# Attention and a mixture of experts on one core: a GpSimd drain in mid-run, row stores by SyncE, and a fixed order in the small experts

## The chip, the cores and the metric

One core of a Trainium2 chip runs the whole program. Its engines are TensorE (matmuls, PE in the profile; PEld are its weight loads), VectorE (DVE), ScalarE (ACT), GpSimd (POOL) and SyncE (SP), each with an instruction queue of its own that runs in order; they wait for each other through semaphores. DMAs are issued by SyncE and GpSimd. The metric is the device time of the program in microseconds.

## The reference

What is computed, cut to what matters: capped softmax attention over 8 x 12 heads with 448 rows of 64, then a mixture of 8 experts in which each of the 3584 rows goes to one expert.

```python
scores = cap * np.tanh(scale * q @ k.T / cap)
attn = softmax(scores)                        # per batch (8) and head (12), 448 x 448
x = (attn @ v), heads side by side            # 3584 rows of 768
logits = x @ w_gate + modality_bias[modality_id]
e_idx = np.argmax(logits, axis=1)
gate_w = softmax(logits)[row, e_idx]
for e in range(8):
    mask = e_idx == e
    h = np.maximum(x[mask] @ w1[e], 0.0)      # 768 -> 1024
    out[mask] = gate_w[mask, None] * (h @ w2[e])   # 1024 -> 768
```

## The kernel before

**Attention** (`attention`, lines 428 to 751) goes over 24 pairs of head pairs, `d`, with seven steps `s` each. A step has scores on TensorE, Tanh and Exp on ScalarE, sums of the weights on DVE, and the products with v on TensorE some steps later. Nearly all of it is pinned: `pin` keeps an instruction at its place in the program order of its engine. At the first step of a pair `fetch(d + 1)` queues three loads of 448 KB each (k and q twice, v once) on SyncE. In the fifth step `tokens(d - 3)` transposes a finished pair, scales it into the tile `xs`, and stores it to the DRAM tensor `xd` (line 580). Of these 24 stores 23 are issued by GpSimd and one, pair 20, by SyncE; the calls for the last two pairs (lines 745 and 746) name GpSimd themselves. GpSimd also writes the row map of the experts with indirect DMAs (line 282).

**Experts.** Rows are gathered per expert in blocks ("slots") of up to three tiles of 128 rows. A slot is `run_slot`: GpSimd gathers the next slot's rows (`gather`, line 801), `ffn1` multiplies with w1 for f = 0 to 7, `ffn2` with w2, ScalarE scales the result (line 940), and GpSimd stores each tile of rows with an indirect DMA (line 949). Weights come in as float32 through four buffers `raw` and are split into a high part (cast on ScalarE, line 820) and a low part (subtraction on DVE, line 821), which are single tiles per k (w1: `ah`, `al`; w2: `bh`, `bl`). A matmul is done as three products of such parts.

With these inputs there are eight slots of three tiles, then the branch of `finish` with slots of 2, 2 and 1 tiles. In a slot of fewer than three tiles (`n < TW`) ffn1 puts the high and the low part of the rows side by side, so that a PSUM bank holds two halves; `finish(ph, f)` inside ffn1 adds them into the tile `acc` (copy at line 885, sum at 886), applies Relu (887) and takes the low part (888). In these slots the w2 splits are called after ffn1 and are not pinned; the order in which they stand among ffn1's instructions is that of the scheduler. The splits of the next slot's w1 are pinned.

**End.** Behind the last store every engine executes a drain and a barrier (line 1219 in the profile, written by the framework); the same at the start has line 1211.

Of the kernel before, what the change touches and what calls it, by code (L numbers as in the profile page):

```python
# [66 lines left out]
FIXED = 7  # L67
# [15 lines left out]
class Program:  # L83
# [344 lines left out]
    def attention(self, firsts, rp, xp):  # L428
        tc, nc = self.tc, self.nc
        pe, pin, V = nc.tensor, self.pin, nc.vector  # L430
        with ExitStack() as st:
# [126 lines left out]
                        rec[:, i].unsqueeze(3).to_broadcast([CP, C, 2, E]), op=ALU.mult,  # L558
                    ))

            def tokens(d, queue=nc.gpsimd, *banks):
                xT, rec = kept.pop(d), recs[d]
                xs = xp.tile([CP, C, 4 * D], F32, name="xs", bufs=2)
                if banks:
                    tps = [pool.tile([128, 512], F32, name="tp", tag=tag) for pool, tag in banks]
                else:
                    tp = ps_x.tile([128, 2, 512], F32, name="tp", tag="xT")
                    tps = [tp[:, i] for i in range(2)]
                for i in range(2):
                    for c in range(C):  # L570
                        pin(pe.transpose(
                            tps[i][:CP, c * 128 : (c + 1) * 128], xT[:, i, c * CP : (c + 1) * CP], self.ident
                        ))
                dst = xs.rearrange("p c (i j d) -> p i c j d", i=2, j=2)
                norm = rec.unsqueeze(4).to_broadcast([CP, 2, C, 2, D])
                for i in range(2):
                    src = tps[i][:CP].rearrange("p (c j d) -> p c j d", c=C, j=2)
                    pin(V.tensor_tensor(dst[:, i], src, norm[:, i], op=ALU.mult))
                b, r = divmod(d, NU)
                put = queue.dma_start(  # L580
                    self.xd[b * S : (b + 1) * S, r * 4 * D : (r + 1) * 4 * D].rearrange("(p c) f -> p c f", c=C), xs
                )
                if queue is nc.sync:
                    self.last_sp = pin(put).ins
# [239 lines left out]
        for k in range(KC):  # L824
            self.split_w(self.load_raw(e, self.w1, k, FF), self.w1s[k], pin=True)

    def load_w2(self, e, raws=(), ks=range(FC), minus=None):
        for k in ks:
            raw = raws[k] if k < len(raws) else self.load_raw(e, self.w2, k, DM)
            self.split_w(raw, self.w2s[k], pin=bool(raws), minus=minus)  # L830

    def move(self, k, pt, n=TW):
        for t in range(n):
# [15 lines left out]
        self.move(k, pt, n)  # L849
        self.take(k, pt, n)  # L850

    def ffn1(self, n, hooks=None):

        nc = self.nc
        w = n * 128
        hh, hl = self.h
        bank = lambda: self.ps_h.tile([128, 512], F32, name="ph")
        lead = LEAD if hooks else 0

        def parts(k):  # L860
            hi, lo = self.w1s[k]
            for a, c in ((hi, 0), (lo, 0), (hi, 1)):
                for f in range(lead):
                    self.pin(nc.tensor.matmul(
                        phs[f][:, :w], a[:, f * 128 : (f + 1) * 128], self.x[:, k, c, :w],
                        start=k == 0 and a is hi and c == 0, stop=k == KC - 1 and c == 1,
                    ))

        def products(ph, f, k):
            hi, lo = self.w1s[k]  # L870
            keep = self.pin if hooks and f <= lead else (lambda inst: inst)
            fs = slice(f * 128, (f + 1) * 128)
            first, last = k == 0, k == KC - 1
            if n == TW:
                keep(nc.tensor.matmul(ph[:, :w], hi[:, fs], self.x[:, k, 0, :w], start=first, stop=False))  # L875
                keep(nc.tensor.matmul(ph[:, :w], hi[:, fs], self.x[:, k, 1, :w], start=False, stop=False))  # L876
            else:
                nc.tensor.matmul(ph[:, : 2 * w], hi[:, fs], self.x[:, k, :, :w], start=first, stop=False)
            keep(nc.tensor.matmul(ph[:, :w], lo[:, fs], self.x[:, k, 0, :w], start=False, stop=last))  # L879

        def finish(ph, f):
            acc = ph[:, :w]
            if n < TW:
                acc = self.op.tile([128, 256], F32, name="acc", bufs=2)[:, :w]
                nc.vector.tensor_copy(acc, ph[:, w : 2 * w])
                nc.vector.tensor_tensor(acc, ph[:, :w], acc, op=ALU.add)
            nc.scalar.activation(hh[:, f, :w], acc, AF.Relu)  # L887
            nc.vector.scalar_tensor_tensor(hl[:, f, :w], acc, 0.0, hh[:, f, :w], op0=ALU.max, op1=ALU.subtract)  # L888

        def hook(*at):  # L890
            if hooks and at in hooks:
                hooks[at]()

        if lead:
            hooks["start"]()
            phs = [bank() for _ in range(lead)]
            for k in range(KC):
                parts(k)
                if k < KC - 1:
                    hook("k", k)  # L900
            for f in range(lead):
                finish(phs[f], f)
            hook("k", KC - 1)
        for f in range(lead, FC):
            ph = bank()
            for k in range(KC):
                products(ph, f, k)
            finish(ph, f)
            hook("f", f)

    def ffn2(self, mt, n, between=(), wait=0, then=None):

        nc = self.nc
        between = list(between)
        for t in range(n):
            ot = self.op.tile([128, DM], F32, name="ot")
            rows = slice(t * 128, (t + 1) * 128)
            pys = {}

            def products(half, f):  # L920
                if f == 0:
                    pys[half] = self.ps_y.tile([128, 512], F32, name="py")
                cs = slice(half * HALF, (half + 1) * HALF)
                for i, (a, c) in enumerate(((0, 0), (0, 1), (1, 0))):
                    nc.tensor.matmul(  # L925
                        pys[half][:, :HALF], self.h[a][:, f, rows], self.w2s[f][c][:, cs],
                        start=f == i == 0, stop=f == FC - 1 and i == 2,
                    )

            both = wait and t == 0  # L930
            if both:
                for f in range(FC):
                    for half in range(2):
                        products(half, f)
            for half in range(2):
                if not both:
                    for f in range(FC):
                        products(half, f)
                cs = slice(half * HALF, (half + 1) * HALF)
                put = nc.scalar.mul(ot[:, cs], pys[half][:, :HALF], mt[:, t, 1:2])  # L940
                if both:
                    self.pin(put)
                    if half:
                        then()
                left = 2 * n - 1 - (2 * t + half)
                if 2 * t + half >= wait:
                    for _ in range(-(-len(between) // left) if left else 0):
                        between.pop(0)()
            nc.gpsimd.indirect_dma_start(  # L949
                self.out, bass.IndirectOffsetOnAxis(ap=mt.bitcast(I32)[:, t, 0:1], axis=0), ot, None,  # L950
                bounds_check=NT - 1, oob_is_err=False,
            )

    def run_slot(self, cur, n, ahead=None, raws=(), hooks=None):

        moves = []  # L960
        if hooks:
            work = hooks[("f", 3)]
            hooks[("f", 3)] = lambda: (work(), self.load_w2(cur[0], raws, range(W2_FIRST, W2_EARLY)))
        elif n == TW:
            self.load_w2(cur[0], raws)
        nxt = ahead() if ahead and not hooks else None
        self.ffn1(n, hooks)
        if hooks:
            self.load_w2(cur[0], raws, range(W2_EARLY, FC))
            nxt = ahead()  # L970
        if n < TW:
            self.load_w2(cur[0], raws)
        then = lambda: self.load_w1(nxt[0])
        if nxt:
            if not hooks:
                then()
            pool = lambda k: (self.ps_h, "ph") if hooks and k % 3 == 2 else (self.ps_t, "ptr")
            moves = [lambda k=k: self.transpose(k, *pool(k), n=nxt[2]) for k in range(KC)]
        self.ffn2(cur[1], n, between=moves, wait=3 if hooks else 0, then=then if hooks else None)
        return nxt  # L980

    def run_slots(self, cur, hooks):
# [4 lines left out]
        def ahead(i, n=TW):  # L987
            meta = self.meta
            if i == 0:
                maps.append(self.second)  # L990
                maps.extend(self.rows(meta, s, flex=s >= FIXED, after=self.got) for s in range(1, FIXED + 3))
            else:
                self.gather(maps[i], n)
            return self.expert(meta, i), maps[i], n

        for i in range(FIXED + 1):
# [227 lines left out]
```

## Time and profile before

| | us |
|---|---|
| median of 3 runs | 857.93 (856.28 to 858.07) |
| the profiled execution | 859.21 |
| its span, first to last instruction | 857.5 |
| TensorE busy | 831.3 |
| ScalarE busy | 532.2 |
| DVE busy | 509.0 |
| GpSimd busy | 147.0 |

The span is shorter than the time of the same execution by what lies around the first and last instruction. Busy time counts compute and GpSimd's DMA issues, no waits, drains, branches or semaphores; an engine can hold up the end in an instruction that isn't counted. In a timeline row the first number is the start in us from the start of the span, the second the duration, and the bracket at the end is the idle time of that engine just before, with what ended it. The attention stage lasts until about 330 us, the slots of three tiles until 754 us, the small ones from there.

### The profile page before, as it was taken

What the parts mean: (1) busy time and instruction counts of PE and PEld (TensorE: products, weight loads), DVE (VectorE), ACT (ScalarE), POOL (GpSimd) and SP (SyncE); (2) the same over time, 40 slices, a digit from 0 to 9 for tenths busy, and PEclk for the clock granted to TensorE, in tenths of its full rate; (3) what the DMA queues carried; (4) which work ended last, traced back from release to release, by engine and by line L of the source; (5) the groups of instructions that cost most, each with busy time, mean ns of one, the idle gap of its engine ahead of it and who ended that gap; (6) DMA issues with size and microseconds to landing.
All of it is one profiled execution on the core that took longest, in us unless ns stands there. A gap on an engine that the chain in (4) does not pass through costs nothing. (4 is left out here: it accounts for less than half of the span.)

```text
span 857.5 us, 15780 instructions
## 1 busy us (share of the span) xinstructions
PE 831.3 (97%) x6176; PEld 630.9 (74%) x6176; DVE 509.0 (59%) x880; ACT 532.2 (62%) x627; POOL 147.0 (17%) x154
## 2 busy tenths in 40 slices
PE   7999999999999989999999999999999999999995
PEld 2344434444434436999999999999999999989984
DVE  3677788877688788954433444443344423466851
ACT  6999999999999876364434434443344433456541
POOL 2000330033032230352020210203012030111000
PEclk9999999999999999999999999999999999999998
DMA  5344445365445674397352564634547353457640
GB/s 173 103 152 128 131 127 171 134 173 116 145 120 139 173 168 174 86 330 262 122 184 106 169 231 141 210 105 162 194 141 250 107 160 134 160 178 237 218 160 6
DMA packets 44388, 136.84 MB, mean 160 GB/s; under 512 B 8638, under 2 KB 9214, under 8 KB 44304
## 3 DMA queue, kind: packets, MB, share of 16 engines
q1 hardware_dynamic: 34576, 101.00, 36.8%
q0 software_dynamic: 9584, 34.74, 12.9%
q8 instruction: 50, 0.82, 0.4%
q14 instruction: 34, 0.28, 0.1%
q10 hardware_dynamic: 144, 0.00, 0.0%
HBM read 114.20 MB, written 22.69 MB: 160 GB/s over the span
## 5 line engine op out<-in xcount | busy, mean ns | idle before, releaser
L466 ACT ACTIVATE pt<-sc,isc 128x896 f32<-128x896 f32 x168 | 160.2, 996 | 14.6 <-PE sc L462 12.1
L925 PE MATMUL py<-bh,hh 128*128 128x384 f32 x464 | 160.0, 345 | 1.3 <-ACT hh L887 1.2
L879 PE MATMUL ph<-x,al 128*128 128x384 f32 (+2 forms) x510 | 160.0, 314 | 0.0
L925 PE MATMUL py<-bh,hl 128*128 128x384 f32 x464 | 156.4, 337 | 0.0
L925 PE MATMUL py<-bl,hh 128*128 128x384 f32 x464 | 156.3, 337 | 0.0
L469 ACT ACTIVATE pt<-pt,cabs 128x1792 f32<-128x1792 f32 x84 | 150.4, 1790 | 2.7
L492 PE MATMUL xT<-pt,va 64*64 64x448 f32 x1344 | 143.1, 540 | 3.5 <-issue 3.5
L480 DVE TENSOR_TENSOR tot<-tot,pt 128x896 f32<-128x896 f32 x120 | 130.3, 1086 | 7.8 <-ACT pt L469 4.6
L875 PE MATMUL ph<-x,ah 128*128 128x384 f32 x366 | 122.7, 335 | 1.2 <-DVE hl L888 1.1
L876 PE MATMUL ph<-x,ah 128*128 128x384 f32 x366 | 122.4, 334 | 0.0
L821 DVE TENSOR_TENSOR bl<-raw,bh 128x768 fp32r<-128x768 f32 x88 | 81.6, 955 | 51.6 <-ACT bh L820 51.5
L492 PEld LDWEIGHTS xT<-pt,va 64*64 64x64 f32 x1344 | 50.0, 133 | 82.6 <-issue 77.8
L820 ACT CAST bh<-raw 128x768 fp32r<-128x768 f32 x88 | 70.6, 841 | 52.5 <-DMA raw<-in_w_dram 49.8
L949 POOL DMA_INDIRECT out_dram<-ot,mt x29 | 32.0, 1102 | 382.1 <-ACT ot L940 310.0
L879 PEld LDWEIGHTS ph<-x,al 128*128 128x128 f32 x510 | 96.0, 188 | 0.0
L887 ACT ACTIVATE hh<-ph 128x384 fp32r<-128x384 f32 x64 | 30.2, 488 | 103.9 <-PE ph L879 99.0
L940 ACT ACTIVATE ot<-py,mt 128x384 f32<-128x384 f32 x58 | 33.6, 580 | 95.8 <-issue 49.9
L925 PEld LDWEIGHTS py<-bh,hh 128*128 128x128 f32 x464 | 87.0, 188 | 2.4 <-ACT hh L887 1.8
L821 DVE TENSOR_TENSOR al<-raw,ah 128x1024 fp32r<-128x1024 f32 x64 | 76.3, 1222 | 20.9 <-ACT ah L820 20.6
L925 PEld LDWEIGHTS py<-bh,hl 128*128 128x128 f32 x464 | 87.1, 188 | 0.1
L925 PEld LDWEIGHTS py<-bl,hh 128*128 128x128 f32 x464 | 87.1, 188 | 0.0
L845 DVE TENSOR_TENSOR x<-ptr,x 128x384 fp32r<-128x384 f32 (+2 forms) x63 | 31.0, 515 | 87.2 <-ACT x L844 82.6
(173 smaller groups left out, 1024.0 us busy)
## 6 DMA issues: line engine op xcount, KB each, us to landing
raw<-in_w_dram SPq DMA_DIRECT2D x88, 384.0 KB
raw<-in_w_dram SPq DMA_DIRECT2D x62, 512.0 KB
kq<-in_kq_dram SPq DMA_DIRECT2D x24, 448.0 KB
va<-in_v_dram SPq DMA_DIRECT2D x24, 448.0 KB
kx<-in_kq_dram SPq DMA_DIRECT2D x24, 448.0 KB
xd<-xs POOLq DMA_DIRECT2D x23, 448.0 KB, 6.2
raw<-in_w_dram POOLq DMA_DIRECT2D x2, 512.0 KB
spare<-in_w_dram POOLq DMA_DIRECT2D x2, 512.0 KB, 8.6
```

What stands on the lines that cost most here:

```text
L466: pin(nc.scalar.activation(weights(n), sc[:, :, :S], AF.Tanh, scale=self.isc))
L469: pin(nc.scalar.activation(pt, pt, AF.Exp, scale=self.cabs))
L480: pin(V.tensor_tensor(tots[d], pt_of(n - 1) if s == 1 else tots[d], pt_of(n), op=ALU.add))
L492: pin(pe.matmul(self.xT[j * D : (j + 1) * D, i, :S], vas[d][rows, o : o + D], pt[rows, j], start=s == 0, stop=s == STEPS - 1,))
L820: keep((cast.tensor_copy if cast else self.nc.scalar.copy)(hi, raw))
L821: keep((minus or self.nc.vector).tensor_tensor(lo, raw, hi, op=ALU.subtract))
L875: keep(nc.tensor.matmul(ph[:, :w], hi[:, fs], self.x[:, k, 0, :w], start=first, stop=False))
L876: keep(nc.tensor.matmul(ph[:, :w], hi[:, fs], self.x[:, k, 1, :w], start=False, stop=False))
L879: keep(nc.tensor.matmul(ph[:, :w], lo[:, fs], self.x[:, k, 0, :w], start=False, stop=last))
L925: nc.tensor.matmul(pys[half][:, :HALF], self.h[a][:, f, rows], self.w2s[f][c][:, cs], start=f == i == 0, stop=f == FC - 1 and i == 2,)
L940: put = nc.scalar.mul(ot[:, cs], pys[half][:, :HALF], mt[:, t, 1:2])
L949: nc.gpsimd.indirect_dma_start(self.out, bass.IndirectOffsetOnAxis(ap=mt.bitcast(I32)[:, t, 0:1], axis=0), ot, None, bounds_check=NT - 1, ...
```

## The change

- `tokens` has SyncE as its default queue instead of GpSimd. Its store is then pinned in SyncE's order.
- In the slot after the fixed eight (`i == FIXED + 1`) GpSimd executes a drain right behind the gather for the next slot.
- In slots of one or two tiles: the first four w2 tiles are loaded and split ahead of ffn1; the splits of the other four are called inside `finish` for f = 0 to 3, between sum and Relu, and pinned; the copy into `acc` goes from DVE to ScalarE; copy, sum, Relu and subtraction are pinned.
- In the last tile of the last slot the scaling of the second half is cut in two, one half by ScalarE and one by DVE.

```diff
-            def tokens(d, queue=nc.gpsimd, *banks):
+            def tokens(d, queue=nc.sync, *banks):
...
-    def load_w2(self, e, raws=(), ks=range(FC), minus=None):
+    def load_w2(self, e, raws=(), ks=range(FC), minus=None, pin=False):
         for k in ks:
             raw = raws[k] if k < len(raws) else self.load_raw(e, self.w2, k, DM)
-            self.split_w(raw, self.w2s[k], pin=bool(raws), minus=minus)
+            self.split_w(raw, self.w2s[k], pin=pin or bool(raws), minus=minus)
...
         def finish(ph, f):
             acc = ph[:, :w]
+            keep = self.pin if n < TW else (lambda inst: inst)
             if n < TW:
                 acc = self.op.tile([128, 256], F32, name="acc", bufs=2)[:, :w]
-                nc.vector.tensor_copy(acc, ph[:, w : 2 * w])
-                nc.vector.tensor_tensor(acc, ph[:, :w], acc, op=ALU.add)
-            nc.scalar.activation(hh[:, f, :w], acc, AF.Relu)
-            nc.vector.scalar_tensor_tensor(hl[:, f, :w], acc, 0.0, hh[:, f, :w], op0=ALU.max, op1=ALU.subtract)
+                keep(nc.scalar.copy(acc, ph[:, w : 2 * w]))
+                keep(nc.vector.tensor_tensor(acc, ph[:, :w], acc, op=ALU.add))
+            if f < len(inside):
+                inside[f]()
+            keep(nc.scalar.activation(hh[:, f, :w], acc, AF.Relu))
+            keep(nc.vector.scalar_tensor_tensor(
+                hl[:, f, :w], acc, 0.0, hh[:, f, :w], op0=ALU.max, op1=ALU.subtract
+            ))
...
-                put = nc.scalar.mul(ot[:, cs], pys[half][:, :HALF], mt[:, t, 1:2])
+                cut = HALF // 2 if last and t == n - 1 and half else HALF
+                put = nc.scalar.mul(ot[:, half * HALF :][:, :cut], pys[half][:, :cut], mt[:, t, 1:2])
+                if cut < HALF:
+                    nc.vector.tensor_scalar(
+                        ot[:, half * HALF + cut :], pys[half][:, cut:HALF], mt[:, t, 1:2], None, op0=ALU.mult
+                    )
...
-        self.ffn1(n, hooks)
+        inside = ()
+        if n < TW:
+            self.load_w2(cur[0], (), range(W2_EARLY))
+            inside = [lambda k=k: self.load_w2(cur[0], (), (k,), pin=True) for k in range(W2_EARLY, FC)]
+        self.ffn1(n, hooks, inside)
...
-        if n < TW:
-            self.load_w2(cur[0], raws)
...
                 self.gather(maps[i], n)
+                if i == FIXED + 1:
+                    self.pin(nc.gpsimd.drain())
```

`W2_EARLY` is 4, `FC` is 8, `HALF` is 384, `FIXED` is 7 and `TW` is 3.

## Rows read from the trace of the kernel before

**Rows 1.** Stages: us, busy PE, PEld, DVE, ACT, POOL, then clock, DMA, GB/s.
```profile
100.00:200.00 100.00, 99.80 (x1010) 41.34 (x1006) 80.01 (x150) 98.22 (x85) 22.84 (x22) 1.00 0.49 146
...
440.00:480.00 40.00, 40.00 (x236) 39.94 (x235) 19.77 (x25) 17.43 (x27) 4.49 (x4) 1.00 0.58 191
...
760.00:800.00 40.00, 39.08 (x228) 35.88 (x227) 31.31 (x55) 22.99 (x37) 3.92 (x4) 1.00 0.79 264
800.00:840.00 40.00, 37.95 (x249) 36.35 (x248) 27.02 (x58) 19.83 (x37) 1.99 (x2) 1.00 0.42 144
```

**Rows 2.** Timeline of TensorE, from the first and last small slot.
```profile
776.51 0.44 PE L925 MATMUL py<-bh,hh 128*128 128x384 f32 x1 [0.92 <-ACT hh L887]
...
828.47 0.22 PE L879 MATMUL ph<-x,al 128*128 128x128 f32 x1
828.52 0.34 PE L878 MATMUL ph<-x,ah 128*128 128x256 f32 x1
828.70 0.22 PE L879 MATMUL ph<-x,al 128*128 128x128 f32 x1
829.68 0.36 PE L878 MATMUL ph<-x,ah 128*128 128x256 f32 x1 [0.77 <-DVE acc L886]
...
832.22 0.35 PE L878 MATMUL ph<-x,ah 128*128 128x256 f32 x1 [0.95 <-DVE acc L886]
...
834.12 0.35 PE L878 MATMUL ph<-x,ah 128*128 128x256 f32 x1 [0.33 <-DVE acc L886]
```

**Rows 3.** Timeline of ScalarE, same two slots.
```profile
775.09 1.05 ACT L820 CAST ah<-raw 128x1024 fp32r<-128x1024 f32 x1 [1.22 <-PE py L925]
776.04 0.41 ACT L887 ACTIVATE hh<-acc 128x256 fp32r<-128x256 f32 x1
...
829.84 0.83 ACT L820 CAST bh<-raw 128x768 fp32r<-128x768 f32 x1 [1.50 <-DMA raw<-in_w_dram]
```

**Rows 4.** Timeline of all engines at the end of the run.
```profile
846.78 0.34 PE L925 MATMUL py<-bh,hl 128*128 128x384 f32 x1
847.15 0.58 ACT L940 ACTIVATE ot<-py,mt 128x384 f32<-128x384 f32 x1 [3.64 <-PE py L925]
848.01 0.98 POOL L949 DMA_INDIRECT out_dram<-ot,mt  x1 [21.31 <-POOLq L1008]
```

**Rows 5.** Line 1219: count, ns (least/median/most), first and last start.
```profile
L1219 POOLq DRAIN  x3: 50/109/5757, 850.9 to 857.2; - x3
L1219 SPq DRAIN  x3: 7/7/13, 851.4 to 856.9; - x3
```

**Rows 6.** Line 1211, the start of the program, same columns.
```profile
L1211 POOLq DRAIN  x1: 183/183/183, 0.5 to 0.5; - x1
```

**Rows 7.** Groups by line on GpSimd: count, busy us, mean ns, idle before.
```profile
L282 POOL DMA_INDIRECT mapd<-pay,pos x32 | 47.8, 1495 | 103.8 <-DVE pos L278 52.5 <-DVE xs L578 35.6 <-DVE early L311 8.3
L801 POOL DMA_INDIRECT xg<-xd,mt x30 | 36.7, 1224 | 38.2 <-PE ptr L834 20.8 <-DMA mt<-mapd 10.2 <-PE py L925 4.3
L949 POOL DMA_INDIRECT out_dram<-ot,mt x29 | 32.0, 1102 | 382.1 <-ACT ot L940 310.0 <-ACT x L844 50.2 <-POOLq L1008 21.3
L580 POOL DMA_DIRECT2D xd<-xs x23 | 16.7, 732 | 127.5 <-DVE xs L578 83.2 <-DVE lg L556 42.8 <-issue 1.2
L792 POOL DMA_DIRECT2D mt<-mapd x6 | 3.3, 550 | 2.8 <-issue 2.8
```

**Rows 8.** Timeline of GpSimd in the first small slot.
```profile
759.37 1.33 POOL L801 DMA_INDIRECT xg<-xd,mt  x1 [0.31 <-issue]
782.08 1.17 POOL L949 DMA_INDIRECT out_dram<-ot,mt  x1 [21.38 <-ACT x L844]
```

**Rows 9.** Line 580, the row stores: us from issue to landing.
```profile
DMA to landing us min/median/max: 5.6/6.2/6.7
```

**Rows 10.** Timeline of SyncE's queue in attention.
```profile
174.00 0.99 SPq L95 DMA_DIRECT2D kq<-in_kq_dram  x2
```

**Rows 11.** Timeline of TensorE, the first use of that load.
```profile
187.44 1.68 PE L462 MATMUL sc<-kq 64*64 64x448 f32 x16
```

More of the change, by code (lines that the diff above doesn't have):

```diff
@@ L850, in transpose, with ffn1 @@
         self.take(k, pt, n)
-    def ffn1(self, n, hooks=None):
+    def ffn1(self, n, hooks=None, inside=()):
         nc = self.nc
@@ L909, in ffn1, with ffn2 @@
             hook("f", f)
-    def ffn2(self, mt, n, between=(), wait=0, then=None):
+    def ffn2(self, mt, n, between=(), wait=0, then=None, last=False):
         nc = self.nc
@@ L978, in run_slot @@
             moves = [lambda k=k: self.transpose(k, *pool(k), n=nxt[2]) for k in range(KC)]
-        self.ffn2(cur[1], n, between=moves, wait=3 if hooks else 0, then=then if hooks else None)
+        self.ffn2(cur[1], n, between=moves, wait=3 if hooks else 0, then=then if hooks else None, last=n < TW and not nxt)
         return nxt
```

## Prediction

> **What bounds the kernel now.** I read the table by stage first. From 100 us to 760 us TensorE is the engine that is never free: it is busy for 99.80 of 100 us in attention and 40.00 of 40 us in an expert of three row tiles [rows 1]. ScalarE is nearly as full in attention (98.22 of 100 us), so neither GpSimd nor SyncE sets the pace there. What the change touches lies mostly behind 760 us, where TensorE has 0.92 us of idle time in one stretch of 40 us and 2.05 us in the next [rows 1]. So second I looked for TensorE's idle time there. It is four stalls: 0.92 us ahead of a product of the second layer at 776.51, and 0.77, 0.95 and 0.33 us in the expert of one row tile [rows 2]. Third, the waits around them: at 776.51 TensorE waits for the Relu of the last f, which ran on ScalarE at 776.04 only because a cast of the next expert's w1 stood ahead of it at 775.09, and that had itself waited 1.22 us [rows 3]. In the last expert a product waits for the DVE sum `acc`, so the order in the ACT and DVE queues sets those stalls, not their load.
>
> Fourth, the end. The last matmul starts at 846.78, ScalarE scales the rows from 847.15 on, GpSimd issues the last store at 848.01 [rows 4]; yet the span is 857.5 us. No engine is busy in what is left; it is filled by GpSimd's DRAIN of 5757 ns that begins at 850.9, after SyncE's wait for that store [rows 5]. This is the largest single wait at the end that no useful work fills.
>
> **Part 1, the drain.** The drain in front of the kernel's work, with no DMA issued by GpSimd before it, took 183 ns [rows 6]; the two after the long one took 109 and 50 ns [rows 5]. The long one is the only drain with GpSimd's DMAs ahead of it: 32 + 30 + 29 + 23 in the four large groups and 14 in five small ones (6, 3, 2, 2, 1), 128 together [rows 7]. If the drain looks after each DMA issued since the one before, it costs 5757 / 128 = 45 ns for each; that is an estimate from these rows. The new drain stands behind the two gathers that end at 759.37 + 1.33 = 760.7, and GpSimd's next instruction is at 782.08: 21.4 us of idle time [rows 8]. Of the 128 DMAs 21 go to SyncE (part 2), and 6 come after the new drain (five stores and one gather), so it has 101 to look after: 101 x 45 ns = 4.5 us, and it may have to wait until the gathers have landed. For that I take the 6.2 us of a row store [rows 9], which makes some 11 us of the 21.4 that cover it. Behind it on GpSimd stand only a store, which waits for ScalarE until 782.08 anyway [rows 8], and the next gather. Without that cover it would hold the gather, and past that the next transposes. The last drain then has 6 x 45 ns = 0.3 us left. What is late next is SyncE, whose own drain comes at 851.4 [rows 5]; now the release comes at 850.92 + 5.76 = 856.68. So it gives 856.7 - 851.5 = **5.2 us**. The bounds are 0 (the time is paid for every drain behind a DMA) and 5.3. I take the upper one, since drains without DMAs behind the long one cost 0.05 to 0.11 us.
>
> The Trainium skill speaks against a gain here: VectorE: DVE Perf Modes, section "The DRAIN you can't avoid", calls the drains at a program's ends boilerplate of about 12 ns, constant. SyncE's 7 to 13 ns agree with it and GpSimd's 5757 ns does not [rows 5]; by the rule the last drain would hold nothing to win, and the time would be that of the first rival.
>
> **Part 2, the row stores.** 21 of the 24 stores of attention's rows go from GpSimd's queue to SyncE's (one is there already, the last two name GpSimd). GpSimd loses 21 issues of 0.73 us [rows 7], which nothing waits for. SyncE gains 21 issues of about the same length, and each makes it wait for the rows `xs`, with the next pair's k, q and v loads queued behind. The tightest of those are the loads issued at 174.00, whose first use is at 187.44: 13.4 us [rows 10, 11]. Three loads and a store of 448 KB each are 1.8 MB; at the stage's 146 GB/s [rows 1] that is 12.6 us, and the DMA engines are only 0.49 busy at that rate, so it may be half of it. The loads stay in time: 0 us, bounds -0.5 and the second rival. At the handover one w2 load of the first expert moves behind the store of pair 21; it is needed only late in that expert's loop over k: 0 us.
>
> **Part 3, the small experts.** The run ends in experts of 2, 2 and 1 row tiles. The change moves 24 PSUM copies from DVE to ScalarE, starts the first four w2 tiles ahead of ffn1, and fixes the order copy, sum, w2 cast (f 0 to 3 only), Relu, subtraction. Per f ScalarE then has 0.41 for the copy, 0.41 for the Relu and 0.83 for a cast [rows 3], in all 8 x 0.82 + 4 x 0.83 = 9.9 us. TensorE needs 11.0 us for ffn1 even in the smallest expert (48 pairs of matmuls, 0.23 us from 828.47 to 828.70 [rows 2]). So the order fits, and two things follow. The Relu of f = 7 comes before the casts of the next w1, so the stall at 776.51 goes: 0.92 us idle, about 1.1 us late against a regular step. And `acc` no longer stands behind two w2 subtractions, so the three of the last expert go: 0.77 + 0.95 + 0.33 = 2.05 us idle. A matmul that starts at 829.68 instead of 828.75 (0.05 after 828.70, as 828.52 after 828.47 [rows 2]) is 0.93 late, 0.16 more than its idle time, because the busy tail of the one before hides that much; with this for each of the four the stalls are worth 2.97 + 0.64 = **3.6 us**. The bounds: +1 us (new stalls of the same kind, where a cast waits for its raw tile as at 829.84, 1.50 us [rows 3]) and -3.8. I take 3.6, because w2's first four tiles now free their buffers earlier. The w1 casts start some 2 us later than now in exchange; they have until the next expert, 10 us and more.
>
> The last scaling (384 columns, 0.58 us [rows 4]) is cut in two halves of 192 columns on ScalarE and DVE. With 0.41 for 256 columns I take 0.36, which gives 0.2 us, less a second wait of GpSimd: **0.1 us**, bounds 0 and 0.25.
>
> **The sum.** 5.2 + 0 + 3.6 + 0.1 = 8.9 us. Against the profiled execution, 859.21 us, that is 850.3; this one stands 1.3 us over the median of the runs, 857.93, and I take the same difference off that: **849.0 us**.
>
> **Rivals.**
> First: every drain behind DMAs costs the same 5.8 us, whatever went before. Then the new one lies in idle time and wins nothing; 857.9 - 3.7 = 854.2 us. For it: there is only one such row. Against it: nothing in the rows explains a fixed price when an empty drain takes 0.05 to 0.18 us [rows 5, 6].
> Second, the slower side: SyncE's store goes ahead of the k, q and v loads and pushes them. If the 6.2 us of a store [rows 9] come fully ahead of 1.34 MB at 146 GB/s, 9.2 us, that is 15.4 us against 13.4 us [rows 10, 11]: TensorE stalls 2 us in each of ten pairs, 20 us, and the time is 849.0 + 20 = 869 us. It decides from the point where store and loads together take more than 13.4 us. Against it: DMA is half idle in attention [rows 1], and a store that goes first also ends first. The Trainium skill has the mechanism, DMA: Bandwidth & Descriptors, section "Queues, rings and completion order": on one engine a ring is consumed in order, while rings of different issuers take turns. No row here shows which of them the store would delay.
> Third: the fixed order only exchanges the stalls. ScalarE runs in order, so a raw tile that lands late (1.50 us at 829.84 [rows 3]) now holds Relu and the next copy, and TensorE waits for a PSUM bank. Then 3.6 us shrink to nothing: 852.6 us.
> Fourth: the change doesn't do what it says, neither drain nor order gives anything, 857.8 us.
>
> **How the numbers follow.** Forecast 0.50 (848 to 850.5), first rival 0.17, second 0.08, third 0.18, fourth 0.07. A range that reaches from 847.0 (bounds of the sum at their best) to 854.8 (first rival) takes in the forecast, the first and the third, 0.85, less some spread. About 0.2%, 1.7 us, is what a measurement of this kernel tells from no change; faster by more than that 0.85, within it 0.07, slower 0.08.
>
> **What would show it.** Right: a GpSimd drain of 4 to 11 us near 761 and one under 1 us at the end; no TensorE idle time over 0.2 us behind 760; the attention stage as long as before. Wrong: two drains of equal length; TensorE waiting for k and q, or for a PSUM bank that `acc` holds; GpSimd's store of 782 held by the drain.

## The result, and the profile after

| | before | after |
|---|---|---|
| median, us | 858.27 (856.28 to 859.32, 6 runs) | 848.92 (847.59 to 850.75, 6 runs) |
| ratio | | 0.9893, 95% interval 0.9877 to 0.9909 |
| profiled execution, us | 859.21 | 848.29 |
| its span | 857.5 | 846.5 |
| TensorE busy | 831.3 | 828.9 |
| ScalarE busy | 532.2 | 537.9 |
| DVE busy | 509.0 | 502.4 |
| GpSimd busy | 147.0 | 126.9 |

The changed kernel is faster by 9.35 us (by the interval 7.8 to 10.6); 849.0 was forecast. The table by stage, with the columns of [rows 1], shows where:

```profile
100.00:200.00 100.00, 99.80 (x1010) 41.36 (x1006) 80.91 (x151) 98.24 (x85) 15.64 (x13) 1.00 0.51 146
440.00:480.00 40.00, 40.00 (x237) 39.90 (x236) 17.70 (x23) 16.34 (x26) 2.41 (x2) 1.00 0.58 194
760.00:800.00 40.00, 39.57 (x230) 36.33 (x229) 28.05 (x46) 26.32 (x51) 3.38 (x3) 1.00 0.75 250
800.00:840.00 40.00, 40.00 (x265) 39.38 (x265) 21.91 (x42) 21.57 (x47) 2.38 (x2) 1.00 0.40 131
```

Attention is as it was: TensorE busy 99.80 of 100 us, ScalarE 98.24, with 9 fewer DMA issues on GpSimd. In the small experts TensorE's idle time falls from 2.97 us to 0.43 us, which is one new stall, of 0.43 us, in the first of them.

The drains (line, count, ns least/median/most, starts), in the middle of the run and at the end; INC_SWDGE_SEM is an instruction of GpSimd that comes up again below:

```profile
L1007 POOLq DRAIN  x1: 13106/13106/13106, 755.2 to 755.2; - x1
...
L1233 POOLq DRAIN  x3: 50/109/597, 845.0 to 846.2; - x3
L1233 SPq DRAIN  x3: 7/7/13, 845.6 to 845.9; - x3
L1233 POOLq INC_SWDGE_SEM  x1: 1341/1341/1341, 752.6 to 752.6; - x1
```

The last long drain went from 5757 ns [rows 5] to 597 ns; 13106 ns are spent at 755.2 instead. GpSimd's timeline shows that this lies in idle time:

```profile
754.81 1.09 POOL L801 DMA_INDIRECT xg<-xd,mt  x1 [1.61 <-PE ph L878]
756.20 1.40 POOL L801 DMA_INDIRECT xg<-xd,mt  x1 [0.30 <-issue]
778.64 1.33 POOL L959 DMA_INDIRECT out_dram<-ot,mt  x1 [21.04 <-ACT ot L946]
```

The next issue waits for ScalarE until 778.64, as in [rows 8]; the drain is over at 755.23 + 13.11 = 768.34. The profile counts a drain as a wait of the sequencer, so it doesn't show as busy time.

The end of the run, all engines:

```profile
840.51 0.34 PE L930 MATMUL py<-bh,hl 128*128 128x384 f32 x1
840.89 0.42 ACT L946 ACTIVATE ot<-py,mt 128x192 f32<-128x192 f32 x1 [3.65 <-PE py L930]
841.34 0.42 DVE L948 TENSOR_SCALAR ot<-py,mt 128x192 f32<-128x192 f32 x1 [7.53 <-ACT ot L946]
842.04 0.98 POOL L959 DMA_INDIRECT out_dram<-ot,mt  x1 [18.83 <-POOLq L1022]
```

The two halves of the cut scaling don't run side by side: DVE waits for ScalarE's half of `ot`. From the start of the last matmul to the last store it is 1.53 us, against 1.23 before [rows 4].

**Where the profiled pair differs.** From the last store's issue to the release behind the long drain: 848.01 to 856.73 before, 842.04 to 845.68 after, 8.72 against 3.64 us: -5.08. From the first matmul of the small experts to the last one: 754.10 to 846.78 before, 751.16 to 840.51 after, 92.68 against 89.35: -3.33. The tail: +0.30. Together -8.11. The remaining -2.8 us of the pair's 10.92 lie ahead of 754 us, where nothing was forecast: 0.87 by the second pair of attention (TensorE's first scores at 6.75 instead of 7.47), 0.35 at the handover, 1.42 in the second slot of three tiles, 0.31 in a later one, less 0.13 us behind the release and around the span.

### The profile page after: what moved, and what is told of

Its sections match the earlier page's. It is cut to its first block, busy times and chain, and to the rows that moved or that the text cites. A ratio compares the mean times of both kernels' runs of the same rounds, so it can differ in the third digit from the quotient of the medians.

```text
span 846.5 us, 15767 instructions
## 1 busy us (share of the span) xinstructions
PE 828.9 (98%) x6176; PEld 630.7 (75%) x6176; DVE 502.4 (59%) x857; ACT 537.9 (64%) x651; POOL 126.9 (15%) x133
## 3 DMA queue, kind: packets, MB, share of 16 engines
q0 software_dynamic: 6896, 25.10, 9.2%
## 5 line engine op out<-in xcount | busy, mean ns | idle before, releaser
L946 ACT ACTIVATE ot<-py,mt 128x384 f32<-128x384 f32 (+1 forms) x58 | 33.5, 578 | 92.3 <-PE py L930 46.5
L891 DVE SCALAR_TENSOR_TENSOR hl<-ph,hh 128x384 fp32r<-128x384 f32 x64 | 34.8, 555 | 80.5 <-ACT hh L890 80.3
```

Of the source, the lines that this page charges most:

```text
L891: keep(nc.vector.scalar_tensor_tensor(hl[:, f, :w], acc, 0.0, hh[:, f, :w], op0=ALU.max, op1=ALU.subtract))
L946: put = nc.scalar.mul(ot[:, half * HALF :][:, :cut], pys[half][:, :cut], mt[:, t, 1:2])
```

## Experiments

Theory: the price of GpSimd's drain goes with the DMAs that it issued since the last one (45 ns each, as forecast), the stores cost nothing, and the fixed order brings the rest. Rivals: a fixed price of 5.8 us, or one by what GpSimd's DMAs moved (6896 of 9584 packets are left to its queue, 4.1 us); stores that push the loads; an order that only exchanges stalls. The first four kernels take the change apart. The medians of before differ a little from one comparison to the next, and the ratios with their intervals can differ from the quotient of the medians by up to 0.1%.

**The stores alone.** Before, with one edit:

```diff
-            def tokens(d, queue=nc.gpsimd, *banks):
+            def tokens(d, queue=nc.sync, *banks):
```

> The row stores alone: 21 of GpSimd's 128 DMAs go to SyncE, no drain in mid-run, the old order in the small experts. Theory A (the last drain looks after each DMA that GpSimd issued since the drain before it; 5.757 us for 128 and 0.597 us for 6 give 42 ns each and 0.34 us on top): 107 DMAs, last drain 4.9 us, and the time falls by that 0.9 us, to about 857.4. Rival B (a fixed price for a drain that has DMAs ahead of it): 5.8 us, time 858.3. Rival C (it goes by packets, not by DMAs: 6896 of 9584 packets are left): last drain 4.1 us, time 856.7. Attention itself: pair starts within 0.3 us of the kernel before once the difference at its start is taken off. If the stores are also the cause of the 1.4 us that the first expert with its w2 in one burst gained (a stall of 1.48 us at 401 in the kernel before, none in the changed one), that stall is gone here and the time is 1.4 us lower still; if the stall is a matter of a single execution, it may stand here as well.

Measured: 860.41 us (858.02 to 863.76) against 857.55, ratio 1.0034 (1.0013 to 1.0055): slower by 2.9 us. Its stretch of attention, columns of [rows 1]:

```profile
100.00:200.00 100.00, 99.81 (x1010) 41.35 (x1006) 80.08 (x150) 98.21 (x85) 14.80 (x13) 1.00 0.51 146
```

and its drains at the end, columns of [rows 5]:

```profile
L1219 POOLq DRAIN  x3: 46/109/8861, 849.0 to 858.4; - x3
```

In attention nothing is pushed: the 24 pairs start within 0.07 us of those of before, from 7.47 to 310.28 us. The second rival falls. The loss is the drain: 8861 ns with 107 DMAs ahead of it, where 5757 ns stood with 128. None of the three prices allows for that.

**The drain alone.** Before, with the drain:

```diff
                 self.gather(maps[i], n)
+                if i == FIXED + 1:
+                    self.pin(nc.gpsimd.drain())
```

> The drain in mid-run alone. Theory A: the last drain has 6 DMAs to look after and takes 0.6 us, the drain in mid-run lasts about 14 us and nobody waits for it; the time falls by 5.1 us to 853.2. Rival B (fixed price): 5.8 us at the end again and 858.3. Rival that the drain in mid-run holds up GpSimd: the store at 782 starts later than ScalarE's last scaling, TensorE waits in the next expert, and less than 5 us is won.

Measured: 852.18 us (850.27 to 853.44), ratio 0.9923 (0.9894 to 0.9951). The drain in mid-run took 9.57 us and held nothing: GpSimd's next issue, at 779.52, waits for ScalarE as in [rows 8]. Those at the end (same columns):

```profile
L1221 POOLq DRAIN  x3: 50/109/597, 849.0 to 850.2; - x3
```

5.757 - 0.597 = 5.16 us is what the trace shows of the drain; the medians differ by 5.4 us. The fixed price falls.

**The order alone.** The changed kernel with stores and drain as before, and without the cut of the last scaling.

> The fixed order in the experts of one or two row tiles alone, with the last scaling in one piece on ScalarE; stores, drain as before. Theory: the stalls of the kernel before in these experts go (2.97 us idle, 3.6 us), and one new stall of 0.7 us stands in the first of them, where ScalarE waits for the fifth and sixth raw tile of w2: 3.3 us from the start of the first small expert to the last matmul, 89.4 against 92.7 us; time 855.0. Rival (the gain came with the stores, which change when w2's tiles land): under 1.5 us, time 857.

Measured: 853.57 us (852.38 to 855.05), ratio 0.9947 (0.9930 to 0.9964): by the medians 4.0 us less. The small experts take 89.95 us instead of 92.68, that is 2.73 us in the trace. The last drain is 5758 ns again, as with the same 128 DMAs it should be. Over all thirteen traces the small experts take 88.58 to 89.95 us in the seven kernels with the fixed order and 92.57 to 95.12 us in the six without, so what one pair of traces gives for the order carries 1 to 2 us of spread.

**The whole without the cut.**

```diff
-... last=n < TW and not nxt)
+...)
```

> The changed kernel with the last scaling in one piece on ScalarE again. The profile of the changed kernel shows the two halves one after the other (0.42 us on ScalarE, then 0.42 us on DVE, which waits for ScalarE). Theory: the cut costs time, 0.87 against 0.58 us from the first scaling's start to the end of the last; without it the last store starts 0.3 us sooner behind the last matmul (1.23 us instead of 1.53 us), time 848.6. My prediction had 0.1 us the other way: the last store 0.1 us later, time 849.0.

Measured: 848.76 us (847.79 to 849.32), ratio 0.9884 (0.9859 to 0.9910), not to be told from the changed kernel by time. The end of its run:

```profile
841.81 0.34 PE L930 MATMUL py<-bh,hl 128*128 128x384 f32 x1
842.19 0.58 ACT L946 ACTIVATE ot<-py,mt 128x384 f32<-128x384 f32 x1 [3.64 <-PE py L930]
843.04 0.98 POOL L959 DMA_INDIRECT out_dram<-ot,mt  x1 [18.61 <-POOLq L1022]
```

1.23 us from matmul to store, as before, and the five other kernels with the order and without the cut have the same 1.23 in their traces. The cut costs 0.3 us.

**What a drain costs.** A price that fits the rows: 8.861 us with 107 DMAs and 0.597 us with 6 give 82 ns for each DMA still open, and 0.1 us. Then before's 5.757 us are 69 DMAs, and 59 of the 128 would have been dealt with during the run. Two kernels test it. One is before with the drain four slots earlier, so that 30 DMAs follow it:

```diff
                 self.gather(maps[i], n)
+                if i == 4:
+                    self.pin(nc.gpsimd.drain())
```

> The kernel before with a GpSimd drain behind the gather of the fourth slot (i == 4) instead of the eighth; 30 of GpSimd's 128 DMAs come after it. By the prediction's price, 45 ns for each DMA since the drain before, the last drain takes 30 x 45 ns = 1.4 us. By a price of 0.1 us and 82 ns for each DMA (the line through 8.861 us for 107 DMAs with the stores moved alone and 0.597 us for 6) it takes 2.6 us, and the 5.757 us of before stand for 69 DMAs, the first 59 having been dealt with in the run. By a fixed price it takes 5.8 us again. The time follows: 857.5 less what the last drain loses, 853.1, 854.3 or 857.5 us.

The other is before with half of the stores moved:

```diff
+                queue = nc.sync if d < 11 else queue
                 xT, rec = kept.pop(d), recs[d]
```

> The kernel before with the row stores of pairs 0 to 10 on SyncE and the others on GpSimd, and no drain in mid-run: 117 DMAs of GpSimd. By 45 ns for each DMA the last drain takes 5.3 us. If each store that leaves GpSimd adds its share of the 3.1 us that 21 stores added, it takes 5.76 + 11 x 0.148 = 7.4 us. If GpSimd's queue deals with its old DMAs only when so many rows have gone through it (as behind some 59 DMAs, 22 stores of 448 rows among them, in the kernel before, and never with the stores moved), that point comes late in the run, few DMAs are left behind it, and the last drain is shorter than before's, 2 to 4 us.

The drains at the end, of the kernel with the early drain:

```profile
L1221 POOLq DRAIN  x3: 50/109/2552, 849.7 to 852.8; - x3
```

and of the one with half of the stores moved:

```profile
L1220 POOLq DRAIN  x3: 50/109/3308, 852.1 to 856.0; - x3
L1220 POOLq INC_SWDGE_SEM  x1: 496/496/496, 754.5 to 754.5; - x1
```

2.552 us where 82 ns for each of 30 gives 2.56: right. With half of the stores moved the drain is *shorter* than with none (5.757) and with all (8.861): 3.308 us, 39 DMAs by the line. So what counts is how many are still open, and something in the run closes the old ones. One execution each: 854.72 us (against 858.13) with the early drain, and 857.87 us with half of the stores moved. There the drain's 2.4 us are taken back in the small experts (95.1 us instead of 92.68), whose order is the unpinned one of before. It isn't idle time: TensorE idles 2.78 us in them, against 2.97 before. Its granted clock falls to half, 1.2 GHz, for 6.8 us from 830.4 on, behind the longest of the stalls (a TensorE row, then a stretch with the columns of [rows 1]):

```profile
829.70 0.35 PE L879 MATMUL ph<-x,ah 128*128 128x256 f32 x1 [1.52 <-DVE acc L887]
...
830.50:837.00 6.50, 6.50 (x33) 6.47 (x31) 4.58 (x14) 2.07 (x5) 0.00 (x0) 0.50 0.02 8
```

When does the queue close them? Counting the rows that each DMA names in the kernel (448 for a row store, 112 for a write of the row map, 384 for three loads of the map, 128 for the others): the first 59 DMAs of before name 13,776 rows, the first 78 = 117 - 39 of the kernel with half of the stores 14,080; with all stores moved the whole run has 14,592 and nothing is closed. That looks like a point a little above 14,592. The next kernel has 16,384 rows in all. (What was expected of it counts 128 for each of the 32 map writes, which name 112; all these sums are some 500 higher that way, and the argument is the same.)

```diff
+                queue = nc.sync if d < 17 else queue
                 xT, rec = kept.pop(d), recs[d]
```

> The kernel before with the row stores of pairs 0 to 16 on SyncE, those of 17 to 19 and 21 to 23 on GpSimd, no drain in mid-run; 111 DMAs of GpSimd, which name 16,896 rows (448 for a row store, mostly 128 for the others). The kernel with all 21 moved has 15,104 rows and 107 open DMAs at the end, the one with 11 moved 19,584 rows and 39 open, before 24,512 rows and 69. If the queue clears its old DMAs when some 16,000 rows have gone through it, as these three would allow, it does so near the end here, and the last drain has some 10 to 25 DMAs open, 0.9 to 2.2 us: 3.5 to 5 us less than before, 853 us, with no drain in mid-run. If it clears only past 16,900 rows, or by something else than rows, the drain is 9.2 us with 111 open, and the time 861 us. By the prediction's 45 ns for each it is 5.0 us.

Its drains at the end and, below them, the instruction INC_SWDGE_SEM:

```profile
L1220 POOLq DRAIN  x3: 50/109/1756, 848.4 to 850.7; - x3
L1220 POOLq INC_SWDGE_SEM  x1: 269/269/269, 752.6 to 752.6; - x1
```

1.756 us, 20 open of 111; the first 91 name 13,824 rows. The time is 852.59 us (851.81 to 853.59), ratio 0.9946 (0.9924 to 0.9969): 5.1 us less than before, without any drain in mid-run, by leaving six stores on GpSimd instead of 23. The drain's part of that is 4.0 us. Here too the granted clock falls to half, for 3.4 us from 828.3 on, behind a stall of 1.65 us. INC_SWDGE_SEM, which GpSimd executes at the branch into the small experts, counts the same thing a second time. It took 1341 ns with 99 open in the changed kernel, and 111 ns right behind the drain of the next kernel, none open: 12.4 ns for each. By that before's 869 ns are 61 open (120 issued by then, less 59), 496 ns are 31 (109 less 78) and 269 ns are 13 (103 less 91 is 12). With the early drain, where the count is known without the price, it took 388 ns, 22 open, and 22 DMAs had been issued since that drain.

That rows are what the queue counts rests on these totals alone. The closed DMAs of the three kernels differ in number (59, 78, 91) and in what they moved (12.9, 15.5 and 20.2 MB), and are alike in rows only; what the queue does at that point no row shows.

**Where the drain stands.** The whole without the cut, with the drain ahead of the gather, so that the gather has to wait for it:

```diff
+                if i == FIXED + 1:
+                    self.pin(nc.gpsimd.drain())
                 self.gather(maps[i], n)
-                if i == FIXED + 1:
-                    self.pin(nc.gpsimd.drain())
```

> The changed kernel without the cut, with the drain in mid-run ahead of the gather instead of behind it. If a drain goes twice over the open DMAs at 41 ns each, the first time while the last of them are still in flight (as the 4.18 us between the gather's landing and the drain's end with 101 open and 2.63 us with 63 say), it takes 0.1 + 99 x 82 ns = 8.2 us here, no gather being in flight; the gathers are issued at some 763.5 and 765, land 8 us later at 773, the first transposes start at 774.2, and the time is that without the cut, 848.8 us. If a drain of this length always takes 13 us, the gathers land at some 778, TensorE stalls 4 us and the time is 852.8 us.

The two drains:

```profile
L1006 POOLq DRAIN  x1: 8819/8819/8819, 752.8 to 752.8; - x1
...
L1233 POOLq DRAIN  x3: 50/109/761, 844.1 to 845.4; - x3
```

The gathers behind it on GpSimd's timeline, and the transpose that needs them on TensorE's:

```profile
762.67 1.21 POOL L801 DMA_INDIRECT xg<-xd,mt  x1 [9.23 <-PE ph L879]
764.19 1.20 POOL L801 DMA_INDIRECT xg<-xd,mt  x1 [0.31 <-issue]
...
772.56 0.47 PE L834 MATMUL ptr<-identr,xg 128*128 128x128 f32 x4
```

8.82 us where 8.2 was expected, and 0.761 us at the end with eight DMAs behind it (0.11 + 8 x 0.082 = 0.76). The gathers go out 8 us later than in the changed kernel. The second has landed at 771.31, the transpose that needs it runs at 772.56: 1.25 us are left of the cover, and TensorE has no idle time there. 847.34 us (847.05 to 847.59), ratio 0.9885 (0.9863 to 0.9908). So the cover holds either way, but here only just.

**Stores back on GpSimd.** The whole without the cut, `queue=nc.gpsimd` again:

> The changed kernel without the cut of the last scaling and with the row stores back on GpSimd: drain in mid-run and fixed order alone. If the stores matter only through the length of the drain, the drain in mid-run takes 9.6 us instead of 13.5, hidden either way, the last one 0.6, and the time is that of the changed kernel without the cut, 848.8 us, within 0.2%. If the stores by SyncE help attention when the last drain doesn't hide it, the time is 0.5 to 1 us above it.

Its drains, in mid-run and at the end:

```profile
L1007 POOLq DRAIN  x1: 11299/11299/11299, 756.2 to 756.2; - x1
...
L1233 POOLq DRAIN  x3: 50/109/597, 845.0 to 846.2; - x3
```

847.59 us (846.66 to 849.39), ratio 0.9877 (0.9857 to 0.9897). The drain in mid-run is 11.3 us, not 9.6, since its second gather landed late (764.86; then 2.63 us to the end, as with the drain alone). The time is not above that with the stores on SyncE. Behind a drain in mid-run these runs tell no difference by the stores.

**The new stall.** In the changed kernel's timeline ScalarE waits in the first small expert:

```profile
757.06 0.83 ACT L820 CAST bh<-raw 128x768 fp32r<-128x768 f32 x1 [1.48 <-DMA raw<-in_w_dram]
757.80 0.41 ACT L890 ACTIVATE hh<-acc 128x256 fp32r<-128x256 f32 x1
...
760.31 0.83 ACT L820 CAST bh<-raw 128x768 fp32r<-128x768 f32 x1 [1.83 <-DMA raw<-in_w_dram]
761.05 0.41 ACT L890 ACTIVATE hh<-acc 128x256 fp32r<-128x256 f32 x1
```

and TensorE behind it:

```profile
762.86 0.50 PE L878 MATMUL ph<-x,ah 128*128 128x512 f32 x1 [0.43 <-DVE acc L887]
```

The raw w2 tiles land late, the pinned cast waits for them, and the Relu and the next copy into `acc` wait behind the cast. The next kernel is the whole without the cut, with the pinned splits two steps later:

```diff
-            inside = [lambda k=k: ... for k in range(W2_EARLY, FC)]
+            inside = [lambda: None] * 2
+            inside += [lambda k=k: ... for k in range(W2_EARLY, FC)]
```

> The changed kernel without the cut, and with the four w2 splits inside ffn1 called for f = 2 to 5 instead of 0 to 3. If the new stall of 0.43 us in the first small expert is ScalarE waiting for raw w2 tiles that have not landed by f = 1 and 2, it goes, and the time is 0.4 us lower than without the cut alone, some 848.4 us. If the order is what counts, a later split holds the last Relu or the second layer and TensorE waits there, 0.5 to 1 us more.

The same casts in its timeline of ScalarE:

```profile
760.28 0.84 ACT L820 CAST bh<-raw 128x768 fp32r<-128x768 f32 x1
761.58 0.84 ACT L820 CAST bh<-raw 128x768 fp32r<-128x768 f32 x1
763.64 0.84 ACT L820 CAST bh<-raw 128x768 fp32r<-128x768 f32 x1
```

The casts no longer wait, the stall is gone and the small experts take 752.53 to 841.19, 88.66 us, instead of 89.35. The median, 848.72 us (847.97 to 849.84, ratio 0.9890, 0.9872 to 0.9909), doesn't show it, and other traces speak against it: with the splits where the changed kernel has them, those of the drain ahead of the gather and of the stores back on GpSimd have no stall and 88.67 and 88.58 us, and that of the whole without the cut has 0.16 us of stall and 89.37 us. The stall comes and goes with the landing of the raw tiles, and what the later call is worth stays open. The last kernel has this and the stores on GpSimd:

> The changed kernel without the cut, with row stores on GpSimd and the w2 splits at f = 2 to 5: what the two earlier kernels had one of each. If each takes away what it seemed to take (the stall of 0.43 us in the first small expert, 0.3 us of the cut), the last matmul comes some 88.6 us after the start of the small experts instead of 89.35, the time is 848 us, below the changed kernel by 0.7 us, which is less than the comparison can tell. Drain in mid-run 11 us, hidden, the last one 0.6.

847.58 us (846.95 to 847.85), ratio 0.9889 (0.9870 to 0.9908); the small experts take 751.53 to 840.18, 88.65 us, no less than with the earlier splits and the stores on GpSimd. The intervals of all these versions cover the changed kernel's ratio, so none is shown to be better; by their traces the cut is worth leaving out (0.3 us).

## Why the prediction was right, step by step

**The drain, -5.2 us forecast, -5.08 in the pair, -5.16 alone.** The size was right and the price wrong. It was right because it hung on the last 5.76 us becoming next to nothing, and six DMAs at 82 ns are 0.6 us where the forecast had 0.3. The step that each DMA issued since the drain before costs 45 ns fails: the stores alone show 8.86 us for fewer DMAs. The price is 82 ns for each DMA still open, and dividing by all 128 hid that 59 of them had been closed. The same step had the drain in mid-run at 11 us instead of 13.1, outside the 4 to 11 us that the forecast named as its sign: the gather landed not 6.2 but 8.0 us after its issue (764.16), and after that it took 4.18 us. What the forecast said would be late next, SyncE's own drain, is: it starts at 845.6, as GpSimd's ends.

The Trainium skill's rule against this gain, VectorE: DVE Perf Modes, section "The DRAIN you can't avoid" (drains at a program's ends are about 12 ns, constant), would have given the first rival's time. SyncE's 7 to 13 ns still agree with it (one of 122 ns stands in the trace with half of the stores); GpSimd's long drain was 597, 761, 1756, 2552, 3308, 5757 and 8861 ns here, so it does not hold for that one.

**The stores, 0 us forecast.** For attention, right: the loads behind the store were in time in all 24 pairs, and the second rival's 20 us were nowhere. As an edit by itself, wrong: +2.9 us, at the far end of the run. The step that failed is "GpSimd loses 21 issues of 0.73 us [rows 7], which nothing waits for". The last drain waits on GpSimd's DMAs that are still open, and by the counts above the 21 stores had brought the queue to the point where it closes the old ones itself. In the changed kernel that cost is in the drain in mid-run, which ends 4.18 us behind the gather's landing with the stores moved and 2.63 us without, and is hidden there.
The Trainium skill advises the move, DMA: Bandwidth & Descriptors, section "SWDGE vs HWDGE vs iDMA": plain transfers belong on SyncE or ScalarE, and those that accumulate, cast or are irregular on GpSimd. No run here shows a gain from it, and one shows a loss.

**The order, -3.6 us forecast, -3.33 in the pair, -2.73 alone.** All four stalls of [rows 2] are gone in the changed kernel. What was missed is the third rival's mechanism in small: the forecast said that w2's first tiles free their buffers earlier, which doesn't help the fifth and sixth tiles, the first that are cast inside ffn1, and it cost 0.43 us of idle time, where the forecast's sign was none over 0.2. The rows show the casts waiting for raw tiles; since the same order ran without a stall in two other traces, the order alone doesn't make it. In the trace of the order alone the small experts lost 0.6 us more than in the changed kernel; whether that comes from the missing drain and stores or from that execution stays open.

**The cut, -0.1 us forecast, +0.3 measured.** Two terms were wrong. "With 0.41 for 256 columns I take 0.36" for 192: ScalarE took 0.42. And two halves side by side: DVE's half waits for ScalarE's, 0.42 + 0.42 + 0.03 = 0.87 us in place of 0.58. The wait is in the row ([7.53 <-ACT ot L946]). Both halves write one tile, `ot`, and read one, `py`; which of the two the wait is for isn't shown, and whether separate tiles would run side by side wasn't tried.

**The sum.** The terms as measured give 5.08 + 3.33 - 0.30 = 8.1 us against 8.9, and from 857.93 that is 849.8. The median came out 848.92, with 8.1 inside the interval of the difference (7.8 to 10.6). The rest of the profiled pair's 10.92 us is not the change's: the 1.42 us of the second slot, where ScalarE waited 2.87 us for a raw tile in the execution of before, are missing as well in the traces of the drain alone and the order alone, where the stores are as before, and mostly in that of the stores alone. The 0.31 us of a later slot are missing in those of the order alone and the stores alone, in that of the drain alone only 0.06 of them. Of the 0.87 us of the start the drain alone and the order alone miss 0.66 and 0.78, and at the handover 0.4 and 0.5. These parts differ from one execution to the next, whatever the edit: the start is like before's, within 0.03 us, in the traces of the stores alone and of the whole without the cut.

Two things more on the numbers. The range's lower end, 847.0, is called the bounds of the sum at their best, but these give 857.93 - (5.3 + 0.5 + 3.8 + 0.25) = 848.1. And no term of the sum has the clock. Of the 43 executions of before that the comparisons list, those with a mean granted clock of 0.990 or less took 858.3 to 862.8 us, and those with 0.994 or more 854.6 to 858.1; the ten of the order alone, with the same long drain at the end, all have 0.993 to 0.995. So the order's 4.0 us by the medians, against 2.73 in the trace, may hold falls of the clock behind the stalls that it takes away, as in the traces with half of the stores and with six stores on GpSimd. The trace of before has none in the small experts, so this isn't shown.

## What to carry to other kernels

A long drain of GpSimd at the end was work that could be put earlier, where GpSimd idles; three places were tried, and each took its part off the end. So set one drain behind the last dense stretch of its DMAs, with the idle time counted as landing time plus the drain's own. Before moving DMAs off GpSimd, look at the last drain, which can grow with fewer DMAs. Before a copy is cut over two engines, look whether both parts share a tile; here the second part waited for the first. And a gain of some tenths of a us that one trace shows is to be looked for in the traces of other kernels with the same code: the later splits' 0.7 us didn't stand that.

## What the runs showed of the hardware that was not expected

- GpSimd's drain takes 0.11 us and 82 ns for each of its DMAs still open: 6 open 0.597 us, 8 0.761, 30 2.552, 107 8.861. At a run's end the last of them had landed when the drain began, or within 0.1 us.
- Half of that falls behind the last landing where the drain starts while DMAs are in flight: 2.63 us with some 63 open, 4.18 with 101, 1.65 with 39; 41 to 42 ns each. That reads as two passes, of which the first runs while the DMAs land. With the drain ahead of the gather it was 6.1 us behind the landing, not 4.1, so the reading isn't complete.
- As worked out above, GpSimd's queue closes its old DMAs by itself, at a point above 14,592 and by 16,384 rows named by them; what is open at the end, and so the last drain, doesn't grow evenly with the number of DMAs: 107 DMAs 8.86 us, 111 1.76, 117 3.31, 128 5.76.
- ScalarE scales 192 columns in 0.42 us and 384 in 0.58: halving the width takes a quarter off the time.
- TensorE's granted clock fell to half (1.2 GHz) behind a stall of 1.52 us in the last expert, for 6.8 us, and behind one of 1.65 us, for 3.4 us. Behind before's stalls (0.95 us at most), and behind one of 1.25 us at 775.8 in the first of these two runs, it stayed at 2.4 GHz.
